# A pooled attention with a token and channel mixer: unit 6's first MLP stage by seven half products, and all steps laid out anew

## The chip, the cores and the metric

The kernel runs on one core of a Trainium2 chip. A core has five engines that run their own instruction queues beside one another: TensorE (PE, matmuls out of SBUF into PSUM), VectorE (DVE), ScalarE (ACT), GpSimd (POOL) and SyncE (SP), of which the last issues DMAs here, as GpSimd does too. The metric is the device time of one execution in microseconds; the figure for a kernel is the median of its timed runs.

## The reference

For 8 batches with 8 heads, 576 rows and head size 64, keys and values are averaged over groups of 8 rows, so that attention goes from 576 rows to 72 pooled ones. The result, 576 x 512 for each batch, goes through a mixer over rows and a mixer over channels, each with a residual.

```python
k_p = k.reshape(B, H, 72, 8, D).mean(axis=3)
v_p = v.reshape(B, H, 72, 8, D).mean(axis=3)
attn = softmax(q @ k_p.T / sqrt(D))              # 576 x 72 for each head
x = (attn @ v_p), heads side by side             # 576 x 512
u = x + (relu(x.T @ w_tok1) @ w_tok2).T          # token mixer, 576 -> 256 -> 576
out = u + relu(u @ w_ch1) @ w_ch2                # channel MLP, 512 -> 1536 -> 512
```

## The kernel before

Matmuls take bf16 operands. The weights stay in SBUF. Of each batch 512 rows make a unit of the channel MLP; the 64 rows left over of every batch are gathered, and these 512 tail rows are unit 8. While the MLP of unit n runs on TensorE, the steps of batch n+1 (scores, attention, token mixer) and the loading and pooling of batches n+2 and n+3 are laid between its matmuls.

The order is written out by hand, and each engine runs its queue in that order. The string HEAD lists the steps of the start. PLAN has one dictionary for each unit. The unit's generator yields 45 times, at fixed points of its matmuls, and the dictionary says which steps are issued after which yield ("step 23" below is the text behind key 23). The steps, b standing for a batch:

- `b.lk`, `b.lv`, `b.lq`: loads (DMAs issued by GpSimd). A DMA of this queue waits, at its issue, for the one eight places ahead of it to land.
- `b.K0`, `b.K1`, `b.V0`, `b.V1`: pooling of half of the heads of k or v on GpSimd, three additions over the 8 rows (L208, L209, then L212 or L214, the result in `kp` or `vp`). In lower case the same on VectorE.
- `b.Q0`, `b.Q1`, `b.kpT`, `b.s0` to `b.s2`: transposes (L312), scores (L325) and their exponentials on ScalarE (L334).
- `b.av0` to `b.av4`: attention times values (L413) for four blocks of rows and the tail block, scaled by the reciprocal on VectorE (L356); `aw` scales on ScalarE (L360). `b.at0`, `b.at1` (L425, L427) and `b.u0` to `b.u4` (L447, and the addition L448 on VectorE): the token mixer.
- `b.t0` and so on: u transposed on TensorE (L456). From batch 3 on, `b.M..` sends u through DRAM by SyncE instead, and `b.T..` transposes what came back in 32 x 32 blocks on VectorE (L490).
- `g`: a gate (L865, L866). VectorE clears a flag and GpSimd copies it, so that GpSimd goes on only when VectorE has come to this point; VectorE's clearing waits for GpSimd's copy of the gate before.

The second stage of the MLP (`GT` times `w_ch2`, L699) is done by seven products of half size, named x, y, z, x2, w, z2 and x3, in the manner of Strassen and Winograd, at yields 24 to 44. They need sums of `GT` (`g_sums`, L579 and L594: `=1` to `=4` on VectorE, with `+` on GpSimd) and sums of the weights (`w0` to `w3`, `weight_sum`). x2 reads the sum of `=2`, w3 and `=4` go into w and z2. Additions at L742 empty the products' banks into s1, s5, s4 and the outputs `o`, which SyncE stores.

The first stage (`u` times `w_ch1`, 24 yields) is plain in units 0 to 6: `l1_tile`, twelve tiles of four matmuls 128x512 (L551), each put through a ReLU into `GT` by ScalarE (L555). In units 7 and 8 it too goes by seven products (`l1_fast`, L672), for three groups A, B and C of four tiles. Each product is four matmuls of 128x256 into half of a PSUM bank. Of the seven, three (5, 1 and 6) are copied out and kept (`keep`, L649), and later products of the same bank are added to what was kept (`add`, L653, with the ReLU at L657 on ScalarE or L659 on VectorE); product 4 is evicted with its ReLU (L685). The order is the string ORDER. This needs sums of `w_ch1`, `Z0` to `Z3` (`ch1_sum`, capital letters on GpSimd, lower case on VectorE), and sums of the transposed u, `y0` to `y3` (`u_sum`, the same). They are kept in buffers of the raw pool, which batches have no more use for.

Four PSUM banks, p1a to p1d, go round by `take` and `give`; two more (`p2`) serve scores and attention. All raw loads of k, v and q come from the pool `raw`, two buffers for each.

Of the kernel before, what the change touches and what calls it, by code (L numbers as in the profile page):

```python
# [35 lines left out]
def kernel(  # L36
# [35 lines left out]
    raw = ctx.enter_context(tc.tile_pool(name="raw", bufs=2))  # L72
# [36 lines left out]
    FAST = [int(t.split(".")[0]) for at in PLAN for v in at.values() for t in v.split() if t[1:] in (".y0", ".Y0")]  # L109
    C1, U1 = [], {}  # L110
# [500 lines left out]
    def ch1_sum(k, eng):  # L611
        a11, a21 = (w_ch1[:, 0:2, i * NH * P:(i + 1) * NH * P] for i in range(2))
        a12, a22 = (w_ch1[:, 2:4, i * NH * P:(i + 1) * NH * P] for i in range(2))
        if k % 2 == 0:
            t = raw.tile([P, 2, 2, NH * P], BF16, name="vr" if k else "kr")
            C1.extend([t[:, 0], t[:, 1]])
        if k == 0:
            eng.tensor_tensor(out=C1[0], in0=a21, in1=a22, op=ALU.add)
        else:
            sub(C1[k], *((C1[0], a11), (a11, a21), (a12, C1[1]))[k - 1], eng)  # L620

    def u_sum(n, k, eng):
        uT = batches[n][2]["uT"] if n < B else uT_tails
        b12, b21, b22 = uT[:, 0:2, hi], uT[:, 2:4, lo], uT[:, 2:4, hi]
        if k == 0:
            U1[n] = raw.tile([P, 4, 2, 256], BF16, name="qb")
        t = U1[n]
        sub(t[:, k], *((b12, uT[:, 0:2, lo]), (b22, t[:, 0]), (b22, b12), (b21, t[:, 1]))[k], eng)

    def l1_fast(n, uT):  # L630
# [9 lines left out]
        def us(k):  # L640
            return lambda kk: U1[n][:, k, kk]
# [3 lines left out]
        bank, kept = {}, {}  # L645

        def keep(g, k):
            kept[g, k] = spare[len(kept) % len(spare)]
            nc.scalar.copy(out=kept[g, k], in_=bank[g, k == 5])  # L649

        def add(g, k, ps, row, half):
            dst = GT[:, half, row * NH + 2 * g:row * NH + 2 * g + 2]
            nc.vector.tensor_tensor(out=dst, in0=ps, in1=kept[g, k], op=ALU.add)  # L653
# [7 lines left out]
        def step(g, k):  # L661
            if k == 1:
                if g > 0:
                    bank[g, 0], bank[g, 1] = (take([P, 2, 256], FP32) for _ in range(2))
                else:
                    bank[g, 0], bank[g, 1] = (ps_two.tile([P, 2, 512], FP32, name="p2")[:, 0].rearrange(
                        "p (j n) -> p j n", j=2) for _ in range(2))
            ps = bank[g, k in (2, 3, 5)]
# [23 lines left out]
    ORDER = "A1 A2 B1 B2 A6 C1 C2 A5 A7 B6 A3 B5 B7 A4 C6 B3 C5 C7 B4 C3 X C4 X X"  # L692

    def unit_fast(n, u):
# [61 lines left out]
        s1, first = keep("s1"), None  # L756
        uT = [u["uT"][:, kk, :] for kk in range(4)]
        if n in FAST:
            step = l1_fast(n, uT)
            for t in ORDER.split():  # L760
                if t != "X":
                    step("ABC".index(t[0]), int(t[1]))
# [7 lines left out]
            for _ in range(3):  # L770
                yield
# [5 lines left out]
        oa, ob = (outp.tile([P, 2, DM], FP32, name="o") for _ in range(2))  # L777
# [8 lines left out]
        s5 = keep("s5")  # L786
# [81 lines left out]
    def unit(n, at):  # L868
# [3 lines left out]
        for i, _ in enumerate(unit_fast(n, st)):  # L872
# [18 lines left out]
    with tc.manual_schedule(engines={PE, POOLE, DVE, ACT, SYNC}):  # L891
# [4 lines left out]
        qb = loaded[0, "q"] = raw.tile([P, HP, BR * D + D], BF16, name="qb")  # L896
# [44 lines left out]
```

## Time and profile before

| what | before |
|---|---|
| timed runs, us | 262.34, 262.4, 263.7; median 262.4 |
| profiled execution, us | 261.59, of which the span 259.8 |
| TensorE matmuls | 253.5 us busy, 2187 instructions |
| VectorE | 195.3 us, 400 |
| ScalarE | 125.1 us, 229 |
| GpSimd | 159.2 us, 166 |
| granted TensorE clock | 0.997 |
| first matmul of units 0 to 8, us | 23.7, 55.6, 85.8, 113.5, 142.9, 167.2, 194.0, 218.6, 237.0 |

Times in the profile count from the start of the span. In timelines the columns are start, duration, engine, line, operation, output and inputs, and in brackets the idle time ahead with what ended it. In groups they are the count, total busy us and mean ns of one, then the idle time ahead. Windows give the length and each engine's busy time and count. Waits give the total, the number of times and the longest.

### The profile page before, as it was taken

The page shows a single profiled execution, that of the slowest core. Times are in us where ns is not written, and L with a number is a line of the kernel's source. Part 1 is how long each engine was busy: PE and PEld are TensorE (multiplying, and loading weights), DVE is VectorE, ACT ScalarE, POOL GpSimd, SP SyncE. Part 2 cuts the span into 40 slices and gives each one's busy share as a digit, 9 for nine tenths or more (in the row PEclk, how much of TensorE's full clock was granted, in tenths as well). Part 3 has the DMA queues.
Part 4 walks back from the last instruction along what each step waited for, and adds up shares of the span by engine and source line. Part 5 has one row for each costly group of instructions (what it writes and reads, how often), then busy time and mean ns, then how long its engine had stood idle before and what let it go on. Part 6 is the DMA issues. An engine that isn't in the chain of part 4 may idle for free.

```text
span 259.8 us, 5518 instructions
## 1 busy us (share of the span) xinstructions
PE 253.5 (98%) x2187; PEld 167.2 (64%) x2187; DVE 195.3 (75%) x400; ACT 125.1 (48%) x229; POOL 159.2 (61%) x166
## 2 busy tenths in 40 slices
PE   8999999999999999999999999999999999999994
PEld 2885456764676645774487447754784478888883
DVE  5557469995789747789799548944795389999993
ACT  3354874059746565466741575065525421623610
POOL 8757226999989999389969962898308913100000
PEclk9999999999999999999999999999999999999998
DMA  7999999994090989479834942930405042503304
GB/s 153 192 201 207 205 207 209 206 225 87 3 174 7 165 192 200 124 132 237 200 109 78 216 170 61 158 97 1 159 20 149 30 146 61 172 0 68 97 3 161
DMA packets 31930, 34.31 MB, mean 132 GB/s; under 512 B 2976, under 2 KB 23968, under 8 KB 31904
## 3 DMA queue, kind: packets, MB, share of 16 engines
q0 software_dynamic: 17856, 17.64, 43.2%
q1 hardware_dynamic: 13632, 15.93, 20.5%
q10 hardware_dynamic: 416, 0.39, 0.5%
q8 instruction: 17, 0.28, 0.4%
q14 instruction: 9, 0.07, 0.1%
HBM read 38.99 MB, written 12.58 MB: 199 GB/s over the span
## 4 chain that ended last, share of the span: by engine, by line
PE 92%; DVE 5%; issue 1%; ACT 0%; DVEq 0%; ACTq 0%
PE p1a L699 8%; PE p1c L551 8%; PE p1d L699 7%; PE p1a L551 7%; PE p1b L699 7%; PE p1b L551 7%; PE p1d L551 7%; PE p1c L699 5%; PE p L413 4%; PE p L325 3%; PE p L672 2%; PE p1d L425 2%; PE p1c L447 2%; PE p1b L425 2%; PE p1b L144 1%; DVE s L742 1%
## 5 line engine op out<-in xcount | busy, mean ns | idle before, releaser
L551 PEld LDWEIGHTS <-w_ch 128*128 128x128 bf16 x336 | 30.2, 98 | 34.0 <-issue 3.0
L699 PEld LDWEIGHTS <-area 128*128 128x128 bf16 x432 | 41.3, 98 | 7.9 <-issue 1.0
L334 ACT ACTIVATE ex<-p 72x768 bf16<-72x768 f32 x42 | 31.6, 803 | 16.1 <-PE p L325 16.1
L866 POOL COPY flag<-flag 1x1 f32<-1x1 f32 x35 | 10.2, 292 | 47.1 <-DVE flag L865 46.9
L699 PEld LDWEIGHTS <-GT 128*128 128x128 bf16 x312 | 29.6, 98 | 7.0 <-issue 1.8
L209 POOL TENSOR_TENSOR t<-t 72x512 f32<-72x512 f32 x22 | 31.0, 1411 | 1.7
L551 PE MATMUL p1c<-uT,w_ch 128*128 128x512 bf16 x92 | 24.9, 379 | 0.0
L208 POOL TENSOR_TENSOR t<-vr 72x1024 f32<-72x1024 bf16 x11 | 24.0, 2181 | 0.6
L208 POOL TENSOR_TENSOR t<-kr 72x1024 f32<-72x1024 bf16 x11 | 24.0, 2178 | 0.3
L551 PE MATMUL p1a<-uT,w_ch 128*128 128x512 bf16 x84 | 22.6, 380 | 0.0
L551 PE MATMUL p1d<-uT,w_ch 128*128 128x512 bf16 x80 | 22.3, 379 | 0.0
L551 PE MATMUL p1b<-uT,w_ch 128*128 128x512 bf16 x80 | 21.5, 379 | 0.0
L356 DVE TENSOR_TENSOR x<-p,den 128x512 bf16<-128x512 f32 x28 | 19.4, 692 | 1.0
L555 ACT ACTIVATE GT<-p1a 128x512 bf16<-128x512 f32 x21 | 12.7, 605 | 14.3 <-issue 7.2
L555 ACT ACTIVATE GT<-p1c 128x512 bf16<-128x512 f32 x23 | 13.9, 603 | 8.1 <-PE p1c L551 8.1
L555 ACT ACTIVATE GT<-p1b 128x512 bf16<-128x512 f32 x20 | 12.1, 604 | 8.8 <-PE p1b L551 5.2
L413 PEld LDWEIGHTS <-ex 72*128 72x128 bf16 x280 | 12.8, 98 | 5.3 <-DVE xt L356 0.7
L555 ACT ACTIVATE GT<-p1d 128x512 bf16<-128x512 f32 x20 | 12.0, 600 | 6.9 <-PE p1d L551 6.1
L579 DVE TENSOR_TENSOR area<-GT 128x1536 bf16<-128x1536 bf16 x9 | 11.0, 1218 | 5.6 <-ACT AT L427 5.1
L413 PE MATMUL p<-vp,ex 72*128 72x65 bf16 x280 | 14.0, 194 | 0.2 <-DVE xt L356 0.2
L448 DVE TENSOR_TENSOR u<-p1c,x 128x512 bf16<-128x512 f32 x11 | 8.0, 730 | 7.9 <-PE p1c L447 7.6
L594 DVE TENSOR_TENSOR area<-GT 128x1536 bf16<-128x1536 bf16 x9 | 9.1, 1016 | 6.1 <-ACT GT L555 5.8
(244 smaller groups left out, 550.3 us busy)
## 6 DMA issues: line engine op xcount, KB each, us to landing
out_dram<-o SPq DMA_DIRECT2D x32, 256.0 KB, 4.1
qb<-in_q_dram POOLq DMA_DIRECT2D x7, 576.0 KB, 10.8
kr<-in_k_dram POOLq DMA_DIRECT2D x6, 512.0 KB, 10.7
vr<-in_v_dram POOLq DMA_DIRECT2D x6, 512.0 KB, 11.7
w_ch<-in_moe_w_ch_dram POOLq DMA_DIRECT2D x5, 512.0 KB, 16.5
mem<-u SPq DMA_DIRECT2D x10, 256.0 KB, 2.2
v<-mem SPq DMA_DIRECT2D x20, 128.0 KB, 2.8
area<-in_q_dram SPq DMA_DIRECT2D x2, 288.0 KB, 3.1
```

The lines of the kernel that those rows point to most:

```text
L208: eng.tensor_tensor(out=t4[:, 0:n], in0=t[:, hs, 0:4], in1=t[:, hs, 4:8], op=ALU.add)
L209: eng.tensor_tensor(out=t4[:, 0:n, 0:2], in0=t4[:, 0:n, 0:2], in1=t4[:, 0:n, 2:4], op=ALU.add)
L334: nc.scalar.activation(out=dst, in_=src, func=AF.Exp, scale=scale)
L356: nc.vector.tensor_tensor(out=dst, in0=view, in1=den[:, :, :, None].broadcast_to([n, a, 4, D]), op=ALU.mult)
L413: nc.tensor.matmul(out=ps[:, h // 4, (h % 4) * (D + 1):(h % 4 + 1) * (D + 1)], lhsT=st["ex"][:, h * S + n0:h * S + n0 + P], rhs=st["vp"][: ...
L425: nc.tensor.matmul(out=ps, lhsT=w_tok1[:, c if c < 4 else 4 + par, m * P:(m + 1) * P], rhs=st["x"][:, c, :] if c < 4 else st["xt"], start= ...
L551: nc.tensor.matmul(out=ps, lhsT=w_ch1[:, kk, m * P:(m + 1) * P], rhs=uT[kk], start=(kk == 0), stop=(kk == 3))
L555: nc.scalar.activation(out=GT[:, :, m, :], in_=ps.rearrange("p (h n) -> p h n", h=2), func=AF.Relu)
L579: eng.tensor_tensor(out=out, in0=a, in1=b, op=ALU.subtract)
L594: eng.tensor_tensor(out=S[0], in0=g[1][0], in1=g[1][1], op=ALU.add)
L699: nc.tensor.matmul(out=ps[i] if split else ps[:, i], lhsT=chunk(u, i, a(m)), rhs=w(m), start=start and m == 0 and (i == 0 or split), stop= ...
L866: nc.gpsimd.tensor_copy(out=flag[:, 1:2], in_=flag[:, 0:1])
```

## The change

Unit 6's first stage becomes fast. Tiles 0, 1, 6 and 7 stay plain (eight half steps "L" in the order), and groups B and C go by seven half products each. The order string now stands in each unit's dictionary under key -1; those of units 7 and 8 are changed a little. A group in lower case has its ReLU on ScalarE. Kept products of unit 6 go into s1, s5, s4 and the halves of the first output tile (`rooms`), those of units 7 and 8 into the old place. The weight sums Z0 to Z3 move from unit 6 into unit 5, the last of them to VectorE. They use the raw k and v buffers of parity 0, the y sums the raw q buffer of parity 0, all free once batch 6 has been pooled and transposed; raw buffers are fixed tiles now, and so are s1, s5, s4 and the outputs. PSUM banks are taken at products 1 and 2 and returned at 3 and 4.

The steps of all units stand at new places, and 32 gates are left of 35. Four steps of unit 0 move to the end of HEAD. 6.V1 and 7.V1 go to VectorE, unit 3's `=4` to GpSimd, 3.av0 and 6.av0 to ScalarE; of the y sums VectorE does six and GpSimd six. Below are HEAD's end, five of the nine dictionaries, and the core of the code.

```diff
-... X2 X3 A2 A3"""
+... X2 X3 A2 A3 0.u1 0.u3 1.kpT 1.Q1"""
 PLAN = [
-    {0: "0.u0 2.lk 0.u1 1.Q0 1.Q1", 2: "1.kpT", 3: "3.lq 2.lq", 5: "0.u3", 6: "1.s0", 7: "0.u2", 8: "2.lv", 9: "1.s1", 11: "1.vpool1", 12: "1.s2 1.vpool0", 13: "=3 g", 14: "1.av2", 15: "1.av1", 17: "1.aw0", 18: "1.av4 g", 19: "w0", 20: "3.lv 1.av3", 22: "w1", 23: "g =1 =2 3.lk", 25: "1.at1 1.at0 =4", 26: "g 2.K1", 27: "2.K0", 28: "w3", 29: "2.V0", 33: "1.u0", 34: "1.u1", 35: "1.u2", 36: "w2", 37: "2.Q1 1.t2", 40: "1.u3", 41: "1.t0", 42: "1.t3", 43: "g 1.t1 3.Q0 2.Q0 1.u4"},
+    {0: "2.lk", 1: "1.Q0 0.u0", 3: "3.lq", 5: "g", 6: "1.s0 0.u2", 9: "1.s1", 10: "1.vpool0 1.vpool1", 12: "=3 1.s2", 13: "2.lq", 15: "1.av2", 16: "1.av1", 17: "g 1.av4 g", 19: "1.aw0 2.lv 3.lk w0", 20: "1.av3", 22: "3.lv", 23: "w1 g =1 =2 =4", 25: "1.at0", 26: "1.at1", 28: "w3", 30: "1.u1", 33: "1.u2", 34: "1.u0", 35: "2.K0 2.K1", 37: "1.t2 w2", 39: "1.u3", 41: "1.t0 2.V0", 42: "1.t3", 43: "1.t1 3.Q0 2.Q0 1.u4"},
-    {0: "2.kpT", 1: "2.v1", 3: "2.s0", 8: "3.K1 2.s2", 9: "3.K0", 11: "4.lq", 12: "2.s1", 15: "3.Q1", 16: "2.aw3", 17: "2.av1", 18: "g", 20: "2.av0", 21: "2.av4", 23: "2.av2 =1", 24: "4.lk", 25: "g", 26: "3.kpT 2.at1", 27: "=2", 28: "2.at0 =4 g", 31: "2.u3 4.Q1", 32: "3.s2", 33: "2.t3 2.u2", 35: "3.s0 3.V1", 36: "=3", 37: "3.V0", 38: "g 2.u1", 39: "4.lv 3.s1 2.u0", 40: "5.lk", 41: "4.Q0 2.t2 2.t0", 43: "2.t1 3.av0 3.av2"},
+    {0: "g 2.kpT", 2: "2.Q1 2.s0", 7: "3.K0 2.s2", 9: "2.v1", 12: "2.s1", 16: "2.aw3", 17: "2.av1", 20: "2.av0", 21: "3.K1 4.lq 2.av4", 23: "2.av2", 24: "4.lk =1", 25: "=3 g", 26: "g =2 2.at1 3.kpT", 28: "3.Q1 2.at0 3.s0", 29: "2.u3 3.V1", 32: "2.u2 =4", 33: "2.t3", 36: "2.t2 3.V0", 38: "3.s2 4.lv 4.Q1", 39: "2.u0", 40: "2.u1 3.s1", 41: "g 2.t1 2.t0", 43: "3.aw0 3.av2", 44: "5.lk"},
 ...
-    {2: "6.K1", 5: "7.lq 7.lk 5.u3", 6: "5.u2", 8: "5.u0", 10: "6.K0", 11: "6.kpT", 12: "5.u1 6.V1 6.V0", 13: "5.M0", 16: "6.s0", 17: "5.M2", 18: "5.M", 20: "7.Q1", 21: "7.Q0", 22: "6.Q1 g", 23: "=1", 24: "6.s1 =3", 26: "g", 28: "=2", 29: "6.s2 5.T1", 30: "g", 32: "g 7.lv 5.T3", 34: "5.T0 =4", 36: "g", 37: "g", 41: "5.T2", 42: "6.av3", 44: "6.av0 5.u4"},
+    {0: "6.K1 5.u0", 1: "7.lk", 2: "5.u2 7.lq", 6: "6.K0", 7: "6.v1", 9: "g 5.u1 5.u3", 10: "5.M2", 11: "6.Q1", 12: "6.V0", 13: "=3", 14: "6.kpT", 19: "7.Q1", 20: "6.s0", 21: "7.Q0", 23: "=1", 24: "5.M0 g", 25: "5.M", 26: "6.s1 =2 g", 29: "5.T1", 31: "g", 32: "5.T3", 35: "=4 6.s2", 36: "7.lv", 37: "g", 38: "5.T2", 39: "6.aw0", 42: "6.av1 5.T0", 44: "5.u4"},
-    {0: "7.K0", 2: "6.av2", 6: "6.av1", 7: "6.av4", 8: "7.K1", 9: "6.at0 7.V1 g", 10: "7.kpT g", 12: "=3", 13: "6.at1 g", 14: "g", 17: "6.u3 7.V0", 18: "6.u1", 20: "g 6.u2 7.s0", 21: "6.u0", 24: "7.s1", 25: "=1", 27: "=2 6.M2", 32: "7.av1", 33: "6.M0 =4", 35: "6.M", 36: "7.s2", 37: "g", 39: "6.T0 6.T2", 40: "g", 41: "6.T3", 42: "6.T1", 44: "7.av2 g 7.av3"},
+    {1: "6.av3 6.av4", 4: "6.av2 Z0 7.K0", 7: "7.K1", 8: "g 7.v1", 10: "6.at0 g", 11: "g =3", 12: "6.at1", 13: "Z1", 14: "6.u1 g 7.V0 7.kpT", 16: "7.s0", 17: "6.u0 6.M0", 18: "6.u2", 21: "g", 22: "6.u3", 23: "=1 6.M2", 24: "6.M", 26: "Z2", 27: "7.s1 =2", 29: "=4", 30: "z3", 33: "7.av1", 34: "7.av2 g", 35: "6.T3 6.T2 6.T0", 37: "6.T1", 38: "g 6.y0", 39: "6.Y1", 40: "7.s2", 44: "g 7.av3"},
-    {1: "Z0", 4: "7.av0", 6: "7.av4", 8: "7.at1", 10: "Z1", 15: "7.at0", 16: "Z2", 17: "7.u1 7.u0 7.M0 7.u3 7.u4", 19: "7.u2", 20: "=3 Z3", 22: "7.M2", 25: "g =1", 27: "=2 7.M", 28: "g", 33: "=4", 34: "g", 35: "g 7.T3", 37: "7.T1 7.M4 7.T2", 38: "7.T0", 42: "7.y0", 43: "g 7.y1", 44: "7.Y2"},
+    {-1: "B1 L L L L B6 L L B2 L L B5 B7 C1 B4 b3 c2 C6 C5 c7 C3 C4", 2: "g 6.y3", 3: "6.y2", 4: "7.av0", 7: "7.av4", 9: "7.at1", 10: "g", 13: "7.at0", 15: "7.u0", 16: "7.u3", 17: "7.u1", 18: "7.u2", 19: "7.M0", 20: "7.u4", 21: "=1", 24: "7.M2", 27: "=2 =3", 28: "7.M4", 29: "=4", 34: "7.M", 35: "7.T0", 38: "7.T2", 39: "7.T3 7.T1 7.y0", 41: "7.Y1"},
 ...
-    FAST = [int(t.split(".")[0]) for at in PLAN for v in at.values() for t in v.split() if t[1:] in (".y0", ".Y0")]
+    FAST = [n for n, at in enumerate(PLAN) if -1 in at]
+    FIRST = FAST[0]
+    raws = {key: [singles.tile([P, n], BF16, name=f"{key}r{i}") for i in range(2)] ...
+    C1 = [raws[key][FIRST % 2][...] for key in "kv" for i in range(2)]
+    U1 = raws["q"][FIRST % 2][:, 0:2048].rearrange("p (s k n) -> p s k n", s=4, k=2)
+    rooms = [s1, s5, s4, outs[0][:, :, 0:256], outs[0][:, :, 256:512]]
 ...
+        t = raws[key][b % 2 if b <= FIRST else 1 - FIRST % 2]
 ...
-    def l1_fast(n, uT):
+    def l1_fast(n, uT, whole):
 ...
-            kept[g, k] = spare[len(kept) % len(spare)]
+            kept[g, k] = stock[len(kept) % len(stock)]      # spare for units 7 and 8, else rooms
 ...
-    ORDER = "A1 A2 B1 B2 A6 C1 C2 A5 A7 B6 A3 B5 B7 A4 C6 B3 C5 C7 B4 C3 X C4 X X"
 ...
+            plain = (x for m in (0, 1, NH, NH + 1) for x in l1_tile(n, m, uT))
+            for t in order.split():
+                if t == "L":
+                    next(plain)
+                    yield
+                    continue
                 if t != "X":
-                    step("ABC".index(t[0]), int(t[1]))
+                    step("abc".index(t[0].lower()), int(t[1]), t[0].islower())
                     yield
```

More of the change, by code (lines that the diff above doesn't have):

```diff
@@ L108 @@
     qT0 = area[:, 3200:3200 + 2 * HP * EV].rearrange("m (a l n) -> m a l n", a=HP, l=2)
-    FAST = [int(t.split(".")[0]) for at in PLAN for v in at.values() for t in v.split() if t[1:] in (".y0", ".Y0")]
-    C1, U1 = [], {}
+    FAST = [n for n, at in enumerate(PLAN) if -1 in at]
+    FIRST = FAST[0]
+    raws = {key: [singles.tile([P, n], BF16, name=f"{key}r{i}") for i in range(2)]
+            for key, n in (("k", H * POOL * D), ("v", H * POOL * D), ("q", HP * (BR * D + D)))}
+    C1 = [raws[key][FIRST % 2][:, i * 4 * BP * NM // 2:(i + 1) * 4 * BP * NM // 2].rearrange("p (a n) -> p a n", a=2)
+          for key in "kv" for i in range(2)]
+    U1 = raws["q"][FIRST % 2][:, 0:2048].rearrange("p (s k n) -> p s k n", s=4, k=2)
+    s1, s5, s4 = (singles.tile([P, 2, 256], FP32, name=name) for name in ("s1", "s5", "s4"))
+    outs = [singles.tile([P, 2, DM], FP32, name=f"o{i}") for i in range(2)]
+    rooms = [s1, s5, s4, outs[0][:, :, 0:256], outs[0][:, :, 256:512]]
     values = [singles.tile([SP, H, D + 1], BF16, name=f"vp{i}") for i in range(2)]
@@ L144, in add_rows, with raw_tile @@
             nc.tensor.matmul(out=part, lhsT=w, rhs=loaded[b, t][:, hs, i, :], start=(i == 0), stop=(i == n - 1))
-    def raw_kv(b, key):
-        t = raw.tile([P, H * POOL * D], BF16, name=key + "r")
+    def raw_tile(key, b):
+        t = raws[key][b % 2 if b <= FIRST else 1 - FIRST % 2]
+        if key == "q":
+            return t.rearrange("p (a n) -> p a n", a=HP)
         if b in WIDE:
@@ L160, in load_q @@
     def load_q(b):
-        qb = loaded[b, "q"] = raw.tile([P, HP, BR * D + D], BF16, name="qb")
+        qb = loaded[b, "q"] = raw_tile("q", b)
         nc.gpsimd.dma_start(out=quarters(qb), in_=q[b].rearrange("(g l) (j n) d -> (l j) g (n d)", l=4, n=2 * BR))
@@ L624, in u_sum @@
         b12, b21, b22 = uT[:, 0:2, hi], uT[:, 2:4, lo], uT[:, 2:4, hi]
-        if k == 0:
-            U1[n] = raw.tile([P, 4, 2, 256], BF16, name="qb")
-        t = U1[n]
+        t = U1
         sub(t[:, k], *((b12, uT[:, 0:2, lo]), (b22, t[:, 0]), (b22, b12), (b21, t[:, 1]))[k], eng)
-    def l1_fast(n, uT):
+    def l1_fast(n, uT, whole):
         def w(i, k):
@@ L640, in us @@
         def us(k):
-            return lambda kk: U1[n][:, k, kk]
+            return lambda kk: U1[:, k, kk]
         factors = {1: (w(0, 0), b(0, lo)), 2: (w(0, 1), b(1, lo)), 3: (ws(3), b(1, hi)), 4: (w(1, 1), us(3)),
@@ L645, in l1_fast, with add @@
         bank, kept = {}, {}
+        wide = (0,) if n >= B - 1 else ()
+        stock = spare if n >= B - 1 else rooms
         def keep(g, k):
-            kept[g, k] = spare[len(kept) % len(spare)]
+            kept[g, k] = stock[len(kept) % len(stock)]
             nc.scalar.copy(out=kept[g, k], in_=bank[g, k == 5])
-        def add(g, k, ps, row, half):
+        def add(g, k, ps, row, half, on_act):
             dst = GT[:, half, row * NH + 2 * g:row * NH + 2 * g + 2]
@@ L654, in add @@
             if g > 0:
-                dst = GT[:, half, row * NH + 4 * (g - 1):row * NH + 2 * g + 2]
-                if g > 1 and k == 5:
+                dst = GT[:, half, row * NH + (0 if g == 1 and whole else 2 * g):row * NH + 2 * g + 2]
+                if on_act:
                     nc.scalar.activation(out=dst, in_=dst, func=AF.Relu)
@@ L659, in add, with step @@
                     nc.vector.tensor_scalar(out=dst, in0=dst, scalar1=0.0, scalar2=None, op0=ALU.max)
[L661 to L668, printed above, removed]
+        def step(g, k, on_act):
+            if k < 3:
+                bank[g, k - 1] = take([P, 2, 256], FP32) if g not in wide else ps_two.tile(
+                    [P, 2, 512], FP32, name="p2")[:, 0].rearrange("p (j n) -> p j n", j=2)
+            ps = bank[g, int(k in (2, 3, 5))]
             a, c = factors[k]
@@ L678, in step, with unit_fast @@
             elif k == 2:
-                add(g, 1, ps, 0, 0)
+                add(g, 1, ps, 0, 0, on_act)
             elif k == 3:
-                add(g, 2, ps, 0, 1)
+                add(g, 2, ps, 0, 1, on_act)
             elif k == 7:
-                add(g, 5, ps, 1, 1)
+                add(g, 5, ps, 1, 1, on_act)
             else:
                 nc.scalar.activation(out=GT[:, 0, NH + 2 * g:NH + 2 * g + 2], in_=ps, func=AF.Relu)
-                if g > 0:
-                    give(bank[g, 1])
-                    give(bank[g, 0])
-        return step
-    ORDER = "A1 A2 B1 B2 A6 C1 C2 A5 A7 B6 A3 B5 B7 A4 C6 B3 C5 C7 B4 C3 X C4 X X"
-    def unit_fast(n, u):
+            if k in (3, 4) and g not in wide:
+                give(ps)
+        return step
+    def unit_fast(n, u, order):
         last = n == B
@@ L754, in first_args @@
             return (lambda m: GT[:, 0, m], lambda m: w_ch2[:, m, lo], True, plus(part(s1), part(x), residual(0, 0)), last)
-        s1, first = keep("s1"), None
+        first = None
         uT = [u["uT"][:, kk, :] for kk in range(4)]
         if n in FAST:
-            step = l1_fast(n, uT)
-            for t in ORDER.split():
+            step = l1_fast(n, uT, "L" not in order)
+            plain = (x for m in (0, 1, NH, NH + 1) for x in l1_tile(n, m, uT))
[4 more added lines that the diff above has]
+                    continue
                 if t != "X":
-                    step("ABC".index(t[0]), int(t[1]))
+                    step("abc".index(t[0].lower()), int(t[1]), t[0].islower())
                     yield
@@ L769, in unit_fast @@
                 yield
-            for _ in range(3):
+            for _ in range(24 + order.count("X") - len(order.split())):
                 yield
@@ L776, in unit_fast @@
         SG, TW = sums_tile("S", "area"), sums_tile("T", "area2")
-        oa, ob = (outp.tile([P, 2, DM], FP32, name="o") for _ in range(2))
+        oa, ob = outs
         if first is None:
@@ L871, in unit @@
         st = batches[n][2] if n < B else dict(uT=uT_tails, u=u_tails, paired=True)
[L872 removed]
+        for i, _ in enumerate(unit_fast(n, st, at.get(-1))):
             for s in at.get(i, "").split():
@@ L895 @@
             nc.sync.dma_start(out=qf[:, a:a + 1, :], in_=q_pairs(a, a + 1))
-        qb = loaded[0, "q"] = raw.tile([P, HP, BR * D + D], BF16, name="qb")
+        qb = loaded[0, "q"] = raw_tile("q", 0)
         nc.vector.memset(qb[:, :, BR * D:], 0.0)
```

16 lines of the change are left out of this document (4 added, 12 removed), and 8 rows, old and new, of the table PLAN.

## The prediction

> **What bounds the kernel now.** I read the page first, then TensorE's waits, then the windows from one unit's first matmul to the next one's, then groups by shape, then single rows. Here are the page's first two lines and its chain, all of TensorE's waits, and the windows of units 0, 1, 4, 5, 6 and 7.
>
> ```profile
> span 259.8 us, 5518 instructions
> ...
> PE 253.5 (98%) x2187; PEld 167.2 (64%) x2187; DVE 195.3 (75%) x400; ACT 125.1 (48%) x229; POOL 159.2 (61%) x166
> ...
> PE 92%; DVE 5%; issue 1%; ACT 0%; DVEq 0%; ACTq 0%
> ```
>
> ```profile
> PE p1a L832 <- DVE area L893: 1.2, 1, 1.2
> PE p L370 <- ACT ex L350: 0.4, 1, 0.4
> PE p L699 <- DVE s L742: 0.2, 1, 0.2
> PE p1b L447 <- DVE flag L865: 0.2, 1, 0.2
> PE p1d L456 <- DVE u L448: 0.2, 1, 0.2
> PE p L413 <- DVE xt L356: 0.2, 1, 0.2
> ```
>
> ```profile
> core 0: us, PE busy (x) PEld busy (x) DVE busy (x) ACT busy (x) POOL busy (x), PEclk, DMA share, GB/s
> 23.70:55.60 31.90, 31.55 (x267) 19.36 (x266) 24.94 (x45) 17.15 (x34) 17.55 (x20) 1.00 1.23 206
> 55.60:85.80 30.20, 29.97 (x297) 18.50 (x296) 23.63 (x38) 20.69 (x40) 28.14 (x28) 1.00 0.46 86
> ...
> 142.90:167.20 24.30, 24.30 (x198) 14.93 (x197) 16.39 (x36) 11.91 (x20) 15.77 (x18) 1.00 0.66 143
> 167.20:194.00 26.80, 26.80 (x236) 16.71 (x235) 17.68 (x43) 13.03 (x21) 15.81 (x18) 1.00 0.28 80
> 194.00:218.60 24.60, 24.60 (x176) 15.26 (x173) 16.65 (x39) 8.25 (x14) 13.11 (x9) 1.00 0.33 97
> 218.60:237.00 18.40, 18.40 (x170) 16.43 (x169) 17.74 (x38) 7.28 (x13) 2.98 (x5) 1.00 0.27 73
> ```
>
> TensorE is the bound: busy for 98% of the span, 92% of the chain, and only 2.4 us of waits, of which 1.2 us is the start. The granted clock is 1.00 in these windows, so nothing is to be had there. TensorE's own work therefore counts in full, and work on another engine counts only where TensorE then waits. The busy time hides part of such waits, because matmul ends are modelled: eight 128x256 matmuls at 109 ns (below) that start at 49.37 are through the array at 50.24, yet the next matmul begins at 50.59. That is 0.35 us lost where the view writes 0.18.
>
> ```profile
> 49.37 1.03 PE L699 MATMUL p1c<-area,GT 128*128 128x256 bf16 x8
> 50.59 0.40 PE L456 MATMUL p1d<-ident,u 128*128 128x128 bf16 x4 [0.18 <-DVE u L448]
> ```
>
> The profiled execution took 261.59 us, span 259.8 and 1.8 around it. The three timed runs are 262.34, 262.4 and 263.7, so the profile lies 0.8 below the median. I work out a difference against the profile and carry it to the median. About 0.5% (1.3 us) is what a measurement of this kernel can tell from no change.
>
> **TensorE's work: -0.79 us.** Unit 6 loses 32 matmuls of 128x512 (tiles 2 to 5 and 8 to 11, four each) and gains 56 of 128x256 (two groups by seven products by four). The rows are the L1 stage of unit 6 (plain) and of unit 7 (half products).
>
> ```profile
> 194.03 1.03 PE L551 MATMUL p1b<-uT,w_ch 128*128 128x512 bf16 x4
> 194.89 1.03 PE L551 MATMUL p1d<-uT,w_ch 128*128 128x512 bf16 x4
> ...
> 218.63 1.04 PE L672 MATMUL p<-uT,w_ch 128*128 128x256 bf16 x8
> 219.50 0.60 PE L672 MATMUL p1d<-uT,w_ch 128*128 128x256 bf16 x4
> ```
>
> From start to start four wide ones take 0.86 us and eight narrow ones 0.87. So 8 x 0.86 = 6.88 goes and 7 x 0.87 = 6.09 comes. This is the only term that reaches the end without conditions.
>
> **Unit 6's VectorE and ScalarE: +0.4 us (0 to 1.2).** New on VectorE are six additions out of PSUM and three ReLUs; on ScalarE six copies and three in-place ReLUs stand where eight evictions stood.
>
> ```profile
> L653 DVE TENSOR_TENSOR GT<-p,ex 128x512 bf16<-128x512 f32 x6 | 3.9, 684 | 0.0
> L659 DVE TENSOR_SCALAR GT<-GT 128x512 bf16<-128x512 bf16 x4 | 1.2, 294 | 0.1
> ...
> 205.12 0.73 DVE L448 TENSOR_TENSOR u<-p1a,x 128x512 bf16<-128x512 f32 x1 [6.40 <-PE p1a L447]
> 205.74 0.73 DVE L448 TENSOR_TENSOR u<-p1d,x 128x512 bf16<-128x512 f32 x1
> ```
>
> VectorE gains 6 x 0.68 + 3 x 0.29 = 5.0 us in unit 6, and 16.65 of its 24.6 us were busy: about 21.7 of 23.8. ScalarE (8.25 busy) has room. The tight place is steps 14 to 20, where the u additions of batch 7 fall among the half products. In VectorE's order stand four L653, five u additions and one ReLU there. Queued operations start 0.62 us apart (205.12, 205.74), so nine take 5.6, with the ReLU 5.9 us. TensorE has seven half products of four (7 x 0.435) and four u products of two wide matmuls (4 x 0.43) there, 4.8 us. VectorE falls behind by up to 1.1 to 1.2 us. TensorE feels it through the banks that the additions empty; one operation's 0.62 of slack lies there, and VectorE was idle for 6.40 us ahead of 205.12 in the kernel before. I take +0.4; the ends are 0 and 1.2. The weight sums need no other cover: they now run in unit 5.
>
> **Sums and pooling moved (units 1 to 5): +0.3 us (-0.3 to +1.3).** Z0 to Z2 stay on GpSimd at 3.1 us each, out of unit 6, and Z3 becomes a VectorE operation of some 0.95. The pooling of half of v goes from GpSimd to VectorE for batches 6 and 7. Only batch 2's v half and one k half ran there.
>
> ```profile
> L618 POOL TENSOR_TENSOR kr<-w_ch 128x1536 bf16<-128x1536 bf16 x1 | 3.1, 3079 | 0.0
> L579 DVE TENSOR_TENSOR area<-GT,area 128x1536 bf16<-128x1536 bf16 x9 | 8.5, 949 | 0.2
> L208 DVE TENSOR_TENSOR t<-vr 72x1024 f32<-72x1024 bf16 x1 | 1.8, 1810 | 0.0
> L209 DVE TENSOR_TENSOR t<-t 72x512 f32<-72x512 f32 x2 | 3.3, 1638 | 0.1
> L214 DVE TENSOR_TENSOR vp<-t 72x256 bf16<-72x256 f32 x1 | 0.8, 835 | 0.0
> ```
>
> Each such pooling is 1.81 + 1.64 + 0.84 = 4.3 us of VectorE. Unit 4 then has 16.4 + 4.3 = 20.7 us of VectorE in 24.3, unit 5 has 17.7 + 4.3 + 0.95 + two short y sums, some 23 in 26.8. On average that is hidden. A block of 4.3 us holds back whatever addition queues behind it: 7.v1 stands before 6.u1, 6.v1 before 5.u1. I put 0.1 on unit 4 and 0.2 on unit 5. The price is the block less the steps until that addition empties a bank that is wanted again: about 1 us each if the order is unlucky. Unit 3's SG4 on GpSimd (3.1 instead of 0.95) is read only 12 steps later: 0.
>
> **The gates: -0.2 us (-0.6 to +1.7).** Three gates go. In unit 0 a gate stood between =4 and GpSimd's pooling of batch 2; now the last one stands ahead of =1, and =1, =2, =4 and w3 follow without one. What happens without a gate is shown in unit 1 (the first two rows, GpSimd and VectorE). The other rows are unit 0 as it ran, GpSimd and then VectorE.
>
> ```profile
> 78.36 2.12 POOL L208 TENSOR_TENSOR t<-vr 72x1024 f32<-72x1024 bf16 x1
> 79.16 2.14 DVE L579 TENSOR_TENSOR area<-GT 128x1536 bf16<-128x1536 bf16 x1
> ...
> 44.00 1.24 POOL L124 DMA_DIRECT2D kr<-in_k_dram  x2 [1.21 <-DMA kr<-in_k_dram]
> 45.42 0.83 POOL L866 COPY flag<-flag 1x1 f32<-1x1 f32 x1 [0.19 <-DVE flag L865]
> 46.22 2.11 POOL L208 TENSOR_TENSOR t<-kr 72x1024 f32<-72x1024 bf16 x1
> ...
> 50.67 2.73 POOL L208 TENSOR_TENSOR t<-kr 72x1024 f32<-72x1024 bf16 x1
> ...
> 43.77 0.96 DVE L579 TENSOR_TENSOR area<-GT,area 128x1536 bf16<-128x1536 bf16 x1
> ...
> 45.26 0.95 DVE L579 TENSOR_TENSOR area<-w_ch,area 128x1536 bf16<-128x1536 bf16 x1
> ...
> 50.44 0.97 DVE L579 TENSOR_TENSOR area<-w_ch 128x1536 bf16<-128x1536 bf16 x1
> ```
>
> The sum that began at 79.16, inside GpSimd's operation of 78.36 to 80.48, ended at 81.30, that is 0.82 after it, and took 2.14 instead of 0.95. At 50.67 it is GpSimd that waits: 2.73 instead of 2.12, behind w2. Whoever comes second waits. In unit 0, though, the gate is not the only thing ahead of the pooling. The same loads are queued before it, and their last issue there waited until 44.00 for batch 2's k to land. In the new order that place, eight issues behind that load, is taken by 3.lv instead of 3.lk. So GpSimd leaves the loads at about 45.2 and its flag copy at 45.5 to 46.1, with =4 (ended at 44.7) done and w3 (begun at 45.26) under way. The pooling then starts after w3, as now. Left is w2: the new order puts the product ahead of it one u product (0.43 and its addition) later, and GpSimd's second half follows at 50.6. Caught there, w2 ends at about 50.6 + 2.1 + 0.8 = 53.5, 1.9 late, and what queues behind it (s4, u3, o0) delays the transposes of batch 1 by some 0.4. Against that, the stalls of 0.35 at 50.59 and of 0.2 at L413, both in unit 0, need not return, since batch 1's u additions now stand three steps sooner. I take -0.2 for unit 0. In unit 1, =3 is moved ahead of that v pooling, which removes the 2.14, and =4 moves towards the next one: 0.
>
> [...]
>
> **No cost.** The four steps moved into the head are TensorE's work at either place. On SP's queue, batch 6's u leaves for DRAM at steps 17 to 24 of unit 5 and is transposed from step 35 on, 11 steps (26.8 / 45 = 0.6 us each) after the last of it, where there were 4. 3.av0 and 6.av0 go to ScalarE, which is half idle. Fixed raw buffers in place of the pool change no instruction.
>
> **The sum.** -0.79 + 0.4 + 0.3 - 0.2 = -0.3 us: 261.3 by the profiled execution, and 262.1 from the median. I forecast 262.1, no change that can be told, with 261.3 to 263.0 as its own range.
>
> **Rivals.**
> Faster (260.5): VectorE keeps up. For it speaks that the fast stages of units 7 and 8 carry more additions and show no wait in the list above. Unit 6 and the moved work then cost nothing. The idle of units 0 and 1 (31.90 - 31.55 and 30.20 - 29.97, 0.58) goes as well, and as the rows at 49.37 show the true loss to be about twice that, 1.1. -0.79 - 1.1 = -1.9. Against it: 4.3 us blocks on VectorE in units 4 and 5, and 5.9 against 4.8 in unit 6.
>
> Slower (264.1): the missing gate. If batch 2's k lands some 0.8 us sooner relative to VectorE, or VectorE comes to w3 that much later, GpSimd's pooling begins ahead of w3 and holds it for up to 2.1 + 0.8 - 0.95 = 2.0 us. The z addition behind it then empties its bank 2.0 late, and TensorE, whose work there is a chain through four banks, loses about 1.8; w2 behind it loses the 0.4 again. It decides at 45.26: GpSimd's flag copy must end before VectorE reaches w3. 262.1 + 0.2 + 1.8 = 264.1. Against it: the wait at 44.00.
>
> No shorter work (262.9): the half products break up the order of weights and run slower than 109 ns in unit 6. The eight in 0.87 us and unit 7's window without idle speak against it; -0.79 would be missing.
>
> **How the numbers follow.** Forecast 0.49, faster 0.24, slower 0.22, no shorter work 0.05. The range takes in the faster rival at 260.5 with 0.2 for scatter and the slower at 264.1 with 0.2: 260.3 to 264.3. Faster by over 1.3 us (under 261.1): 0.20 of the first rival and 0.05 of the forecast. Slower by over 1.3 (over 263.7): 0.19 of the second rival, 0.04 of the forecast and 0.02 of the last. That leaves 0.50.
>
> **What would show it.** Unit 6's window: 24.6 should shrink to about 24.2; at 23.8 VectorE kept up, at 25 it did not. In unit 0, w3 and w2: 0.95 each is the faster rival, w2 at about 2.8 the forecast, w3 above 2 the slower one. TensorE's waits should name u additions or L659's additions (L653 before) near step 18 of unit 6. The forecast is wrong if units 4 and 5 grow by more than 0.5 us, or if unit 0 changes by more than 1.

## The result and the profile after

The changed kernel takes 266.5 us (median of four runs, 266.12 to 266.93), the kernel before 262.37: a ratio of 1.0163, with a 95% interval of 1.0136 to 1.0189. It is 4.1 us slower, outside the range that was given. The ratios here and below leave out two executions that ran longer than the others of their kernel at a lower granted clock: one of e1 (265.14 us, clock 0.991) and one of e8 (325.72 us, clock 0.756).

The first matmuls of units 1, 5, 6 and 7 came at 56.6, 168.0, 199.4 and 223.5 us (55.6, 167.2, 194.0 and 218.6 before). The span grew by 264.3 - 259.8 = 4.5 us: +1.0 up to unit 1, -0.2 in units 1 to 4, +4.6 in unit 5, -0.5 in unit 6 and -0.4 behind it. The loss sits in two places. The lines of the page, then TensorE's waits, then windows of units 5 and 6:

```profile
span 264.3 us, 5582 instructions
...
PE 253.1 (96%) x2189; PEld 169.6 (64%) x2211; DVE 213.4 (81%) x410; ACT 129.9 (49%) x248; POOL 156.3 (59%) x161
```

```profile
PE p1d L699 <- DVE area L588: 2.8, 1, 2.8
PE p1c L456 <- DVE o L739: 1.3, 1, 1.3
```

```profile
168.00:199.40 31.40, 28.47 (x233) 17.42 (x235) 28.17 (x48) 12.95 (x21) 22.40 (x19) 0.95 0.24 67
199.40:223.50 24.10, 23.99 (x198) 17.54 (x197) 20.54 (x45) 9.65 (x17) 1.24 (x4) 1.00 0.32 99
```

There are two new waits of a microsecond or more, one in unit 5 and one in unit 0, and in unit 5's window the granted clock, 1.00 before, has a mean of 0.95. Lines have moved by some numbers: L588 is the old L579, L217 the old L208, L739 the old L742, L659 the old L653, L603 the old L594. Some matmul records are missing from this trace (2189 of 2211). Timelines of GpSimd, VectorE and TensorE in unit 5 (start, duration, instruction):

```profile
184.43 1.27 POOL L218 TENSOR_TENSOR t<-t 72x512 f32<-72x512 f32 x1
185.78 1.33 POOL L223 TENSOR_TENSOR vp<-t 72x256 bf16<-72x256 f32 x1
187.05 0.17 POOL L866 COPY flag<-flag 1x1 f32<-1x1 f32 x1
187.19 3.08 POOL L588 TENSOR_TENSOR vr<-w_ch 128x1536 bf16<-128x1536 bf16 x1
...
182.33 0.06 DVE L865 MEMSET flag<- 1x1 f32 x1 [0.28 <-POOL flag L866]
...
184.59 1.92 DVE L603 TENSOR_TENSOR area<-GT 128x1536 bf16<-128x1536 bf16 x1 [0.39 <-ACT GT L564]
...
187.10 3.98 DVE L588 TENSOR_TENSOR area<-area,GT 128x1536 bf16<-128x1536 bf16 x1
...
191.14 0.61 PE L699 MATMUL p1d<-area,area 128*128 128x256 bf16 x4 [2.77 <-DVE area L588]
...
193.18 2.77 PE L699 MATMUL p1a<-area,GT 128*128 128x256 bf16 x12
195.74 1.26 PE L699 MATMUL p1b<-w_ch,area 128*128 128x256 bf16 x8
```

The gate of step 21 is not what times Z2: VectorE has cleared its flag at 182.33, and GpSimd comes to it only at 187.05, because the pooling 7.V0 lasts until then. GpSimd begins Z2 at 187.19. VectorE's =2 is issued in the same tenth of a microsecond, as the addition before it runs until 187.18. By the start column =2 is even 0.09 ahead; that it came second is read from the lengths, since Z2 takes its usual 3.08 us and =2 takes 3.98 instead of 0.95. It ends at 191.08, 0.81 after Z2's end at 190.27. Below, a sum that waits in this way is called held, or caught. Product x2 has to read =2, so TensorE stands still. After that, twelve matmuls that take 1.47 us in e2's profile below take 2.77.

The sum before, =1 (L603), is held too: it takes 1.92 us and ends 0.81 after the pooling's second addition. In the kernel before, 7.V0 began at 179.50 and was over before =1. Here Z1 stands ahead of it on GpSimd, and it begins at 182.24.

The same in unit 0, GpSimd and then VectorE and TensorE:

```profile
43.93 1.24 POOL L131 DMA_DIRECT2D vr<-in_v_dram  x2 [1.95 <-DMA kr<-in_k_dram]
45.16 0.17 POOL L866 COPY flag<-flag 1x1 f32<-1x1 f32 x1
45.30 2.11 POOL L217 TENSOR_TENSOR t<-kr 72x1024 f32<-72x1024 bf16 x1
...
45.41 2.83 DVE L588 TENSOR_TENSOR area<-w_ch,area 128x1536 bf16<-128x1536 bf16 x1
...
48.88 0.38 PE L456 MATMUL p1c<-AT,w_tok 128*128 128x512 bf16 x1 [1.34 <-DVE o L739]
```

The pooling of batch 2 begins 0.11 us ahead of w3. The sum w3 is held until 0.83 after the pooling's first addition, and TensorE waits for the bank that the next addition empties.

### The profile page after: what moved, and what is told of

The parts are those of the page before. It is cut to its first block, busy times and chain, and to the rows that moved or that the text cites. A ratio compares the mean times of both kernels' runs of the same rounds, so it can differ in the third digit from the quotient of the medians.

```text
span 264.3 us, 5582 instructions
## 1 busy us (share of the span) xinstructions
PE 253.1 (96%) x2189; PEld 169.6 (64%) x2211; DVE 213.4 (81%) x410; ACT 129.9 (49%) x248; POOL 156.3 (59%) x161
## 5 line engine op out<-in xcount | busy, mean ns | idle before, releaser
L560 PEld LDWEIGHTS <-w_ch 128*128 128x128 bf16 x304 | 27.3, 98 | 29.7 <-issue 2.3
L218 POOL TENSOR_TENSOR t<-t 72x512 f32<-72x512 f32 x20 | 28.7, 1434 | 1.6
L217 POOL TENSOR_TENSOR t<-kr 72x1024 f32<-72x1024 bf16 x11 | 23.4, 2123 | 0.4
L217 POOL TENSOR_TENSOR t<-vr 72x1024 f32<-72x1024 bf16 x9 | 19.8, 2204 | 2.4 <-DMA vr<-in_v_dram 2.0
L560 PE MATMUL p1a<-uT,w_ch 128*128 128x512 bf16 x70 | 20.0, 379 | 0.3
L560 PE MATMUL p1c<-uT,w_ch 128*128 128x512 bf16 x72 | 19.8, 379 | 0.1
L560 PE MATMUL p1d<-uT,w_ch 128*128 128x512 bf16 x70 | 19.5, 379 | 0.2
L699 PE MATMUL p1d<-area,area 128*128 128x256 bf16 x84 | 11.7, 277 | 2.8 <-DVE area L588 2.8
L588 POOL TENSOR_TENSOR qr<-uT,qr 128x512 bf16<-128x512 bf16 x3 | 3.7, 1220 | 18.2 <-DVE qr L588 18.1
L588 DVE TENSOR_TENSOR area<-GT 128x1536 bf16<-128x1536 bf16 x9 | 11.9, 1321 | 2.4 <-ACT GT L564 2.4
L369 ACT ACTIVATE x<-p,den 128x64 bf16<-128x64 f32 x48 | 10.5, 331 | 6.1 <-DVE den L426 6.1
```

Source lines behind the costliest of these rows:

```text
L217: eng.tensor_tensor(out=t4[:, 0:n], in0=t[:, hs, 0:4], in1=t[:, hs, 4:8], op=ALU.add)
L218: eng.tensor_tensor(out=t4[:, 0:n, 0:2], in0=t4[:, 0:n, 0:2], in1=t4[:, 0:n, 2:4], op=ALU.add)
L369: nc.scalar.mul(dst[:, a, h], view[:, a, h], den[:, a, h:h + 1])
L560: nc.tensor.matmul(out=ps, lhsT=w_ch1[:, kk, m * P:(m + 1) * P], rhs=uT[kk], start=(kk == 0), stop=(kk == 3))
L588: eng.tensor_tensor(out=out, in0=a, in1=b, op=ALU.subtract)
L699: nc.tensor.matmul(out=ps[i] if split else ps[:, i], lhsT=chunk(u, i, a(m)), rhs=w(m), start=start and m == 0 and (i == 0 or split), stop= ...
```

## Experiments

Theory A is that these two collisions make the loss. Theory B is that VectorE, 81% busy instead of 75%, is simply overfull, so that a wait taken away comes back elsewhere. All times are medians; the kernel before, run beside them, had 262.11, 262.3 and 262.28 in the three sets (e1 to e4, e5 to e7, e8 and e9).

**e1: Z2 later, behind a gate.**

```diff
-  23: "=1 6.M2", 24: "6.M", 26: "Z2", 27: "7.s1 =2", 29: "=4", 30: "z3",
+  23: "=1 6.M2", 24: "6.M", 27: "7.s1 =2", 29: "=4", 30: "z3 g Z2",
```

> The changed kernel with the weight sum Z2 taken out of step 26 of unit 5 and issued after the sums =2, =4 and z3, behind a gate of its own at step 30. Theory A (whichever of GpSimd and VectorE comes second is held): Z2 no longer holds =2, so TensorE's stall of 2.9 us at 188.1 goes, and with it the stretch of about 3.3 us at a granted clock near 0.57, which cost another 1.5. 266.5 - 4.4 = 262.1, within 0.5. Rival B (VectorE in unit 5 is overfull, 22 to 24 us of work in 27): another late operation takes the place of =2 and less than 2 us comes back, 264.5 or more. Rival C (the clock dips for another reason, such as more weight loads): only the stall comes back, 263.6, and the dip stays near 193.

262.34 us, ratio to the kernel before 1.0011 (0.9989 to 1.0033). One step moved gives back about 4.1 us, nearly the whole loss, which decides against theory B for unit 5. The stall at 188 is gone, =2 takes 0.94 us, and the granted clock of its profile is 0.998. The times scatter from 261.12 to 265.14. In its profile, w3 in unit 0 is caught and TensorE waits 2.0 us for it:

```profile
44.75 1.24 POOL L131 DMA_DIRECT2D vr<-in_v_dram  x2 [2.59 <-PE p1a L434]
45.98 0.17 POOL L866 COPY flag<-flag 1x1 f32<-1x1 f32 x1
46.12 2.11 POOL L217 TENSOR_TENSOR t<-kr 72x1024 f32<-72x1024 bf16 x1
...
45.57 3.48 DVE L588 TENSOR_TENSOR area<-w_ch,area 128x1536 bf16<-128x1536 bf16 x1
```

These rows do not fit the plain reading that whoever starts second waits. VectorE was done with the addition before at 45.66, 0.46 ahead of the pooling, and yet w3 ended 0.82 after the pooling's first addition. GpSimd was issuing a load until 45.99. Whether that counts is not shown: in e6's profile w3 ran its 0.95 us under such an issue.

**e2: a gate behind w3.**

```diff
-  26: "1.at1", 28: "w3", 30: "1.u1"
+  26: "1.at1", 28: "w3 g", 30: "1.u1"
```

> The changed kernel with one gate more, behind w3 in unit 0, so that GpSimd's pooling of batch 2 starts after w3 as it does in the kernel before. Theory A: w3 takes 0.95 us instead of 2.83 and TensorE's stall of 1.5 at 47.3 goes. As w2 can then be caught by the second half of the pooling, between 1.0 and 1.5 us come back: 265.0 to 265.5. Rival B: VectorE's queue is late there anyway, no change, 266.3 to 266.7.

265.75 us, 1.0132 (1.0106 to 1.0159): 0.75 us came back, less than the 1.0 expected at least. The stall of 1.5 us is gone, but the pooling of batch 2 now ends later, and a new wait has come at the start of unit 1, where `2.kpT` needs it:

```profile
PE p1d L699 <- DVE area L588: 2.8, 1, 2.8
...
PE p1b L265 <- POOL kp L221: 0.6, 1, 0.6
```

This run also shows the stall without the slow stretch behind it. Its profiled execution took 264.23 us, the five others 265.63 to 266.95. The profile has the same 2.77 us stall in unit 5, but TensorE goes on at full clock (1.00 from 190.5 to 194.5 us):

```profile
190.31 0.61 PE L699 MATMUL p1d<-area,area 128*128 128x256 bf16 x4 [2.77 <-DVE area L588]
...
192.16 1.47 PE L699 MATMUL p1a<-area,GT 128*128 128x256 bf16 x12
```

So one and the same stall is followed by a stretch at a lower clock (0.54 from 192.5 to 196 us in the changed kernel) or not. From the restart behind the stall to unit 6's first matmul it is 7.16 us here (190.31 to 197.47) and 8.28 in the changed kernel (191.14 to 199.42), so the stretch costs 1.1 us there, less than the 1.5 that the expectations took. The times alone would not show it: of the five other executions four have a mean granted clock of 0.987 to 0.992, but one has 1.00 and took 265.75 all the same.

**e3: both.**

> The changed kernel with both: Z2 behind the sums of unit 5 and a gate behind w3 in unit 0. Theory A: the gains add up, 266.5 - 4.4 - 1.3 = 260.8, which is 1.6 us below the kernel before: the half products of unit 6 (0.8 less of TensorE) and the stalls that the new layout removed elsewhere are then what is left. Rival B: the moved work costs about as much as they bring, 262 to 263.

261.61 us, 0.9981 (0.9967 to 0.9995). Two placements make the changed kernel slightly faster than the kernel before. A's 260.8 was not reached: it added up 4.4 and 1.3, and e1 and e2 by themselves brought about 4.1 and 0.75. The waits that are left, and the windows of units 1, 4, 5 and 6:

```profile
PE p1b L265 <- POOL kp L221: 0.6, 1, 0.6
...
PE p1d L699 <- DVE area L603: 0.2, 1, 0.2
```

```profile
55.20:85.90 30.70, 30.07 (x297) 18.38 (x296) 23.38 (x39) 20.65 (x42) 29.34 (x28) 1.00 0.46 90
143.30:167.60 24.30, 24.30 (x199) 14.68 (x197) 19.52 (x39) 13.84 (x28) 15.39 (x15) 1.00 0.71 159
167.60:194.90 27.30, 27.09 (x236) 16.82 (x235) 24.06 (x45) 12.94 (x21) 21.70 (x18) 1.00 0.28 78
194.90:219.00 24.10, 24.10 (x199) 17.56 (x197) 21.56 (x49) 9.55 (x17) 2.11 (x5) 1.00 0.32 99
```

Unit 1 is 0.5 longer than before (30.20), because of kpT, whose input GpSimd now delivers late. Unit 5 is 0.5 longer (26.80): scores of batch 7 wait at 191.9 for a bank that VectorE empties late. The sum =1 of unit 5 is still held (1.92 us), and TensorE's wait for it is the 0.2 above. Unit 4 is as long as before.

**e4: the kernel before, without the gate of step 26 in unit 0.**

```diff
-  25: "1.at1 1.at0 =4", 26: "g 2.K1", 27: "2.K0"
+  25: "1.at1 1.at0 =4", 26: "2.K1", 27: "2.K0"
```

> The kernel before without the gate at step 26 of unit 0, so that GpSimd's pooling of batch 2 follows the issue of its loads (ended at 45.24 in the profile of before) while w3 begins at 45.26. Theory A: whoever is first by some hundredths of a us decides. If the pooling is first, w3 takes about 2.9 us and TensorE stalls for 1.0 to 1.5: 263.4 to 263.9. If w3 is first, nothing changes: 262.4. Rival B (gates cost or save nothing): 262.4 with w3 caught all the same.

263.76 us, 1.0064 (1.0045 to 1.0084). The old kernel gets the new one's collision in unit 0 when this gate alone is taken away:

```profile
45.67 2.14 POOL L208 TENSOR_TENSOR t<-kr 72x1024 f32<-72x1024 bf16 x1
...
45.85 2.79 DVE L579 TENSOR_TENSOR area<-w_ch,area 128x1536 bf16<-128x1536 bf16 x1
```

**e7: half of Z2 at step 26, half behind the gate** (the edit of e2, and Z2 in two instructions).

```diff
-  26: "Z2", 27: "7.s1 =2", 29: "=4", 30: "z3",
+  26: "Z2", 27: "7.s1 =2", 29: "=4", 30: "z3 g Z4",       # Z2: first half of C1[2], Z4: second half
```

> The changed kernel with the gate behind w3, in which only half of Z2 (128x768 of its 128x1536) stays at step 26 of unit 5 and the other half goes behind the gate at step 30. Theory A (held for the whole of the other's instruction): =2 is held for half as long, and TensorE's stall is 2.9 - 1.5 = 1.4 us. Then for the clock: if the granted clock falls only after the longer stall, the time is that of both repairs plus 1.4 us, 263.0, with little scatter. If any stall brings it down, 1.5 more, 264.5. Rival B (it is the place, not the length, that costs): 265.7 as with the whole of Z2.

263.58 us, 1.0053 (1.0033 to 1.0073), all six times between 263.18 and 263.87.

```profile
187.37 1.62 POOL L588 TENSOR_TENSOR vr<-w_ch 128x768 bf16<-128x768 bf16 x1
...
187.28 2.52 DVE L588 TENSOR_TENSOR area<-area,GT 128x1536 bf16<-128x1536 bf16 x1
```

=2 ends at 189.80, 0.81 after the half sum, and TensorE's stall is halved from start to start (1.50 us; 2.94 with the whole Z2). With half the instruction on GpSimd (1.62 us in place of 3.08) =2 loses half as much: it takes 2.52 us in place of 3.98, against 0.95 alone. The granted clock stays at 1.00 (187 to 194 us). The time is 0.6 above the 263.0 that the full clock was to give, and 0.9 below the 264.5 of the other case.

**e5 and e9: unit 6 plain again, with both repairs.** In e5 the sum =1 of unit 6 stood at step 21 and so read the old content of the last plain tile; e9 issues it at step 23.

```diff
-        if n in FAST:
+        if n in FAST and n != FIRST:
...
-  20: "7.u4", 21: "=1", 24: "7.M2"      (e9 alone)
+  20: "7.u4", 23: "=1", 24: "7.M2"
```

> The kernel with both repairs (Z2 behind the sums, a gate behind w3), in which unit 6's first stage is plain again: twelve tiles of four wide matmuls, with all sums and steps left where they are. It prices the half products alone. Theory A (the prediction's terms: 0.8 us less of TensorE, about 0.4 given back to VectorE's additions): 0.3 to 0.6 us slower than with both repairs alone, near 262.1. Rival B (VectorE's additions eat the whole): no difference, 261.6. Rival C (nothing is given back): 262.4.

> As the kernel with a plain unit 6 and both repairs, with the sum =1 of unit 6 moved from step 21 to step 23, behind the last plain tile, whose new value it has to read (at step 21 it read that tile's old one). Theory A: 0.3 to 0.9 us slower than both repairs with the half products, 262.0 to 262.5, and unit 6 takes 24.6 us from its first matmul to that of unit 7, as in the kernel before, against 24.1. Rival B (the moved sum delays the second stage): 0.5 us more than at step 21.

262.26 and 262.04 us, against 261.61 with the half products. Unit 6 in e9:

```profile
194.60:219.20 24.60, 24.60 (x177) 15.23 (x174) 17.42 (x40) 8.36 (x14) 2.11 (x5) 1.00 0.33 97
```

24.6 against 24.1: the half products are worth 0.5 us of unit 6. The medians say 0.4, but they come from different sets, and the intervals of the two ratios overlap (e9 1.0000, 0.9984 to 1.0017).

**e6: tuned.**

```diff
-  23: "w1 g =1 =2 =4", ... 28: "w3", ... 35: "2.K0 2.K1", 37: "1.t2 w2",     (unit 0)
+  23: "w1 g =1 =2 =4 w3", ... 35: "2.K0", 37: "1.t2 w2 g 2.K1",
-  26: "Z2", 27: "7.s1 =2", 29: "=4", 30: "z3",                               (unit 5)
+  27: "7.s1 =2", 29: "=4", 30: "g Z2",
-  3: "6.y2",                                                                 (unit 6)
+  3: "6.y2 z3",
```

> The changed kernel with the two collisions taken away by placing, and two later waits with them: w3 stands right behind =4 in unit 0; the second half of k's pooling stands behind w2 and a gate; Z2 stands behind =4 and a gate in unit 5, and z3 goes to step 3 of unit 6. Theory A: of the stalls left with both repairs, the one of 0.8 us at 55.7 (kpT waits for the pooled k of batch 2) and the one of 0.5 at 191.9 (scores of batch 7 wait for a bank that VectorE empties late) go, 261.6 - 1.2 = 260.4. Rival B: they come back at other places, 261.3 to 261.8.

261.21 us, 0.9999 (0.9962 to 1.0035): inconclusive, since the twelve times fall into groups (seven from 260.80 to 261.37, one of 262.78, four from 263.87 to 264.59). (The expectation of e8 below counts the first group as eight.) In the profile, of the first group, the waits named are gone from the list, as A has it, but the kernel does not keep to that. Three of the four late executions have a mean granted clock of 0.992 or 0.993, all others of this run 0.997 or more, which points to the clock for part of their lateness.

**e8: tuned, with a gate behind w3** (unit 0, step 23: `w1 g =1 =2 =4 w3 g`; z3 at step 10 of unit 6).

> As the tuned kernel, with a gate behind w3 in unit 0 as well, and z3 moved on from step 3 to step 10 of unit 6. The tuned kernel without that gate had eight of twelve times at 260.8 to 261.4 and four at 263.9 to 264.6. Theory A: the four are executions in which the loads landed earlier, so that GpSimd's pooling came ahead of w3 again. With the gate they are gone: all times within 1 us, median 260.5 to 261.0, 0.5% below the kernel before. Rival B (something else than that race splits them): times near 264 remain.

260.75 us, 0.9948 (0.9929 to 0.9968): the fastest kernel of the study, 0.5% below the kernel before. The five times that the comparison uses lie between 260.38 and 261.26, none near 264. That fits the race as the cause of e6's second group. It does not prove it: if a third of all executions were late, as in e6, five in a row would still miss them once in eight; no profile of that group was taken; and z3 was moved too. Unit 5 in its profile:

```profile
167.20:194.10 26.90, 26.90 (x237) 16.75 (x236) 23.67 (x47) 12.94 (x21) 21.97 (x19) 1.00 0.28 79
```

## Why the prediction was wrong

**TensorE's work (-0.79) and unit 6 (+0.4): right in their sum.** Unit 6 was to shrink to about 24.2 and has 24.1, and plain it has 24.6 (e9). The two terms were not measured apart. Start to start, TensorE loses little where VectorE was to be late, at steps 14 to 20; queued additions are spaced by 0.6 us as worked out.

**Sums and pooling moved (+0.3, to +1.3 at most): the step that failed.** It priced the pooling blocks on VectorE and took Z0 to Z2 to be the same 3.1 us on GpSimd at another place. It never asked which VectorE sum each of them meets. In unit 6 Z2 had run from 202.27 to 205.36, ahead of every sum of `GT` there (the first began at 208.56). In unit 5, with Z1 ahead, the pooling 7.V0 ends just when =2 is due, and Z2 follows it. The blocks themselves were sized about right: unit 4 is unchanged in e3, and unit 5 is 0.5 longer in e3 but only 0.1 in e8, where z3 and Z2 are moved away. What was missing is one collision: TensorE starts 2.94 us late by the profile, the clock adds 1.1, and e1 gives about 4.1 back.

**Gates (-0.2, to +1.7): wrong in sign, and it was the rival.** The slower rival named the place, the pooling against w3 in unit 0, and a held w3 2.0 late; w3 took 2.83, which is 1.9 late, and TensorE stood for 1.50 where 1.8 was worked out. It was given only 0.22, and the reason found against it rested on a misread row. The load was where the prediction had it (the issue waited until 43.93 and ended at 45.17). But the flag copy was taken to last 0.3 to 0.9 us, as the 0.83 of the kernel before suggests. There it had been issued under w3 and was itself being held: 45.42 + 0.83 = 46.25, next to w3's end at 46.21. Free, it takes 0.17. So GpSimd was ready at 45.30, and w3 came at 45.41. Nor would the times that the prediction worked out have been safe: in e1's profile GpSimd came at 46.12, 0.55 after w3's start, and w3 was held all the same, which the reading that the later start waits does not explain and which stays open. e2 gives 0.75 back and e4 costs the kernel before 1.65, so the loss is between these, not 1.8; in e2 the pooling that starts later takes part of the gain back at kpT. w2 was expected to be caught and lost 0.5 us (1.49 instead of 0.97), not 1.9.

On how a caught sum is held, the prediction's reading of the row at 79.16 (2.14 us in place of 0.95, its end 0.82 after GpSimd's operation) was right in the main: the held sums shown here ended 0.81 to 0.83 us after the other instruction. The risk of a missing gate was real, though the sum caught was w3, not =4, which kept its 0.96 us. On who is second the trace agrees only in part, as e1's w3 shows.

**The clock: not in the prediction at all.** All its terms took the clock as 1.00. The stretch at a clock of 0.54 (192.5 to 196 us) behind the stall of unit 5 cost 1.1 us.

**Theory B of the experiments** (VectorE overfull) explains at most a part of the rest: of 1.6 us expected below the kernel before in e3, 0.5 came. Of the waits that came in e3, the 0.5 in unit 5 is VectorE's lateness; the 0.8 at kpT, from start to start, is GpSimd's. Placing removed most of both (e8), which moved several steps at once.

## What to carry to other kernels

A 0.95 us sum on VectorE took 2.8 and 4.0 us here when it was held by a GpSimd instruction of 2.1 and 3.1 us. What TensorE loses depends on who needs the sum: 1.5 and 2.9 us there, 0.2 for =1 in e3. All that were held here add two SBUF tiles; additions of a PSUM bank and an SBUF tile kept their length beside the poolings (0.73 us at 183.47 and 0.71 at 50.59 in the changed kernel). So for every GpSimd step that is moved, list the VectorE sums of the held kind that are due within its length, and say what orders them: a gate between them is an order; a margin of 0.1 us is none, and in e1's profile even 0.55 us by the start column was none. A duration read from a profile may itself contain such a wait; before it is used as a price, look at its shortest case (the flag copy: 0.17, not 0.83). Where a change brings a small sure gain along with a new layout, price the layout's worst collision first: it was five times the gain here, and moving one step and adding two gates turned +1.6% into -0.2%.

## What the hardware showed that was not expected

The granted clock fell to about half after a stall in the middle of a busy kernel. Windows of the changed kernel around the stall of unit 5 (columns as before; the granted clock is the third number from the right):

```profile
188.00:191.00 3.00, 0.36 (x4) 0.08 (x1) 3.00 (x1) 0.00 (x0) 2.26 (x1) 1.00 0.51 130
191.00:192.50 1.50, 1.36 (x23) 1.27 (x24) 1.50 (x4) 0.00 (x0) 0.00 (x0) 1.00 0.02 5
192.50:196.00 3.50, 3.50 (x25) 2.56 (x22) 3.43 (x10) 0.00 (x0) 0.15 (x1) 0.54 0.02 5
```

TensorE is back at 191.14 at full clock (1.00 up to 192.6), and only then does it run at about half: the granted clock is 0.50 from 192.9 to 196.0 and 1.00 again from 196.3, and there is one 128x256 matmul every 213 ns instead of 109. The same stall in e2's profile had no such stretch, and half the stall (e7) showed none either. The mean granted clock of whole executions says the same: 0.992 to 0.994 in all four of the changed kernel, 0.987 to 0.992 in four of e2's six and 1.00 in the other two, 0.998 or more in all six of e7.

Ahead of the fall TensorE had waited 2.77 us, 2.94 from start to start, and it was busy before and behind. What brings the clock down after one such stall and not after another is not shown, nor how much idle it takes: behind the 1.5 us of e7, and behind e1's wait of 2.0 us in unit 0, the profiles show a clock of 1.00.
